# Feed-forward layers: a ranked queue behind every six matmuls, no GpSimd there, and attention heads in another order

## The chip, the cores and the metric

The kernel runs on one core of one Trainium2 chip. Its time is the device time of one execution in microseconds (us); a time shown without more is the median of three executions. Everything else comes from one profiled execution of the same program.

## The reference

The kernel computes a masked attention and then two feed-forward layers on its output. `q`, `k` and `v` are 2 x 8 heads x 768 x 64; the mask lets a query see only keys of the same sign bucket.

```python
    mask = q_bucket[:, :, :, None] == k_bucket[:, :, None, :]
    scores = scale * np.matmul(q, k.transpose(0, 1, 3, 2))
    scores = np.where(mask, scores, -1000000000.0)
...
    x = np.ascontiguousarray(attn_out.transpose(0, 2, 1, 3)).reshape(B * S, H * D)
...
    h = x @ w_in                                   # 1536 x 512 @ 512 x 2048
    g = h * (1.0 / (1.0 + np.exp(-1.702 * h)))     # layer 0; layer 1: h * tanh(softplus(h))
    return (g @ w_out).astype(np.float32)          # 1536 x 2048 @ 2048 x 512
```

## The kernel before

**Attention** is a software pipeline of 96 steps (16 heads x 6 query tiles of 128). A step holds, in a fixed order, transposes of the probabilities, the mask's clamp on VectorE, the exponential on ScalarE, the next step's scores and the product with `v`; a dictionary `todo` adds work at given steps. GpSimd prepares each head's operands. When a pair of heads is done, `x_out` (GpSimd) writes its 128 features into `xq`. `norm0` (GpSimd), `norm0b` (VectorE's reciprocal), `norm1` (a TensorE transpose), `norm2` and `norm3` (DMAs) bring a head's row sums to `x_out`. The batches are the token halves; the heads come in order 0 to 15, so that the last batch's pairs of features come as 0, 1, 2, 3.

**Feed-forward** (`moe`) holds f32 values as a high part rounded for the fast matmul format plus a low part, and takes three matmuls (high x high, high x low, low x high) for one product. The tokens are cut in three blocks of 512. Block r goes straight through; the other two, c = 0 and 1, share a Winograd-like scheme: seven products for a 2 x 2 block product in place of eight. Its left factors come from `xq` (`xfactors`: `b11`, `t1`, `t2`, `b21`, `t3`, `b22`, `t4`, each for e = 0, 1 and each split in high and low), its right ones from the weights (`ssums`, `ssplit`: four sums of quarters of the weight tiles, then their split).

The 2048 hidden features are taken in 16 tiles f, two to a pair p. The work on TensorE for a pair comes in units of six matmuls of 512 columns: R1 (four units: hidden tile of block r), R2 (four: its output tiles), Q1 (seven products, each a unit) and Q2 (eight output tiles of blocks 0 and 1), so 23 units or 138 matmuls for a pair and 16 pairs in two layers. After Q1 or R1 come activations on ScalarE, each computed twice (rounded `gh`, full), and `gl`, their difference. An output tile is added to `yr` or `xq` (L749), which frees its PSUM bank, one of three.

The weights arrive as 64-bit words, one tile of 512 KB for each (layer, f, in or out), by the DMA queue of SyncE into three buffers. `wsplit` turns a tile into f32 and splits it: ScalarE (L136, L138), VectorE's shift (L140) and its merge (L143; in layer 1 two instructions, L145 and L146), ScalarE's rounding (L158), and the low part (L160).

All of this is written out by hand, without a scheduler: every engine executes its instructions in the order of the program and waits in place for what the next one needs. Around each group of units `run` spreads a list of background steps evenly over the units, first the units' own hooks and then as many background steps as divide the list evenly. GpSimd does in feed-forward: the low parts of the weights (L160), `ssums` and the low part of `ssplit` (L191), one of seven recombinations of Q1 (`h1`, L815, which also needs a copy by ScalarE, L814), one of four `gl` of Q1 (L725), `xr_lo` (L752), and half of `xfactors`.

The order of a pair from the third on is Q1, R2, R1 of the next pair, Q2. Between the layers all of `xfactors` for both e is put in one block behind R1 of layer 1's first pair.

## Time and profile before

| | |
|---|---|
| median of three executions | 795.69 us (794.42 to 796.49) |
| the profiled execution's own time | 793.73 us |
| its span, first to last instruction | 791.8 us |
| mean granted clock of TensorE | 0.984 |
| busy: TensorE, VectorE, ScalarE, GpSimd | 94%, 67%, 54%, 52% |

Engines are named PE (TensorE), PEld (its weight loads), DVE (VectorE), ACT (ScalarE), POOL (GpSimd) and SP (the DMA queue of SyncE). L749 is line 749 of the kernel. A row of a timeline has start (us from the span's start), duration (us), engine, line, operation, output<-inputs, shape and, in brackets, how long the engine had been idle before it and what ended that. A row of groups has the count, busy us in all, mean ns of one, and after the bar the idle us before them with what ended it. A row of stretches has the stretch, its length, the busy us of PE, PEld, DVE, ACT and POOL (instructions in brackets), the granted clock (1.00 is 2.4 GHz, 0.50 is 1.2 GHz) and the DMA engines' share and rate. Some records of matmuls are missing, and a matmul's end is modelled, so that back-to-back matmuls overlap in the rows.

### The profile page before, as it was taken

How to read it: one execution, taken by the hardware profiler on the slowest of the kernel's cores; microseconds unless marked ns; L12 is line 12 of the kernel's file. 1: busy time of each engine (PE TensorE's matmuls, PEld its weight loads, DVE VectorE, ACT ScalarE, POOL GpSimd, SP SyncE). 2: the span in 40 equal slices, each digit the busy share in tenths (PEclk: the TensorE clock that was granted, in tenths of full speed). 3: DMA queues.
4: the chain of work that ended last, by engine and by line, in shares of the span. 5: the costliest groups of instructions: out<-in, count | busy, mean ns of one | idle time of the engine just before them, and what ended most of it. 6: DMA issues, size and time to landing. Idle time of an engine off the chain costs nothing.

```text
span 791.8 us, 10720 instructions
## 1 busy us (share of the span) xinstructions
PE 745.6 (94%) x3688; PEld 632.8 (80%) x3688; DVE 529.9 (67%) x920; ACT 429.7 (54%) x859; POOL 410.3 (52%) x375
## 2 busy tenths in 40 slices
PE   8999999999998899999999999739989999999998
PEld 7999999999976687778787787527867877778786
DVE  8888888988987625555465545685555657566464
ACT  7888888888885453443434433454433443343421
POOL 8867877788555533424434345474433442434520
PEclk9999999999999999999999999979999999999999
DMA  6666667666332111121121211201111112121004
GB/s 166 171 159 154 155 158 177 164 157 165 98 99 85 49 60 53 40 94 54 54 80 54 81 53 54 92 14 53 55 53 53 60 47 81 54 79 54 27 0 160
DMA packets 25911, 69.60 MB, mean 88 GB/s; under 512 B 4448, under 2 KB 6720, under 8 KB 25856
## 3 DMA queue, kind: packets, MB, share of 16 engines
q1 hardware_dynamic: 25856, 68.91, 30.1%
q8 instruction: 29, 0.48, 0.2%
q14 instruction: 26, 0.21, 0.1%
HBM read 49.19 MB, written 3.19 MB: 66 GB/s over the span
## 4 chain that ended last, share of the span: by engine, by line
PE 61%; DVE 12%; ACT 11%; POOL 8%; issue 8%; DMA 0%; SPq 0%; DVEq 0%; POOLq 0%; ACTq 0%
PE y L737 20%; PE s L448 8%; PE pt L509 8%; PE h L242 5%; PE W L783 4%; PE u L534 4%; PE u L533 4%; PE Y L783 3%; ACT gh L722 2%; PE X L783 2%; DVE gl L725 2%; PE prep L357 2%; POOL wl L160 2%; DVE raw L140 1%; DVE wb L143 1%
## 5 line engine op out<-in xcount | busy, mean ns | idle before, releaser
L160 POOL TENSOR_TENSOR wl<-wb,wh 128x512 fp32r<-128x512 f32 x60 | 79.1, 1319 | 100.2 <-ACT wh L158 100.2
L521 DVE TENSOR_TENSOR ptl<-pt,pth 128x384 fp32r<-128x384 f32 x192 | 98.2, 552 | 24.6 <-ACT pth L516 23.7
L516 ACT CAST pth<-pt 128x384 fp32r<-128x384 f32 x192 | 83.0, 484 | 29.4 <-PE pt L509 29.2
L737 PE MATMUL y<-wh,gh 128*128 128x512 f32 x192 | 77.5, 404 | 21.5 <-ACT yr L747 12.3
L749 DVE TENSOR_TENSOR xq<-xq,y 128x512 f32<-128x512 f32 x112 | 75.0, 684 | 30.4 <-PE y L737 29.1
L472 ACT ACTIVATE p<-p,mn 128x768 f32<-128x768 f32 x96 | 91.1, 949 | 2.3 <-DVE p L461 2.2
L461 DVE TENSOR_SCALAR_CACHE_REDUCE p<-s 128x768 f32<-128x768 f32 x96 | 90.5, 944 | 0.8 <-PE s L448 0.7
L158 ACT CAST wh<-wb 128x512 fp32r<-128x512 f32 x64 | 39.5, 617 | 91.4 <-DVE wb L143 47.0
L725 POOL TENSOR_TENSOR gl<-r,gh 128x512 fp32r<-128x512 f32 x16 | 20.7, 1295 | 128.8 <-ACT r L723 128.8
L737 PE MATMUL y<-gh,wh 128*128 128x512 f32 x192 | 77.1, 402 | 9.4 <-DVE xq L749 6.6
L509 PE MATMUL pt<-ident,p 128*128 128x128 f32 x576 | 80.9, 274 | 0.4 <-ACT p L472 0.3
L737 PE MATMUL y<-gh,wl 128*128 128x512 f32 x192 | 76.3, 397 | 1.8 <-DVE wl L160 1.8
L737 PE MATMUL y<-gl,wh 128*128 128x512 f32 x192 | 76.0, 396 | 0.0
L737 PE MATMUL y<-wh,gl 128*128 128x512 f32 x192 | 76.0, 396 | 0.0
L737 PE MATMUL y<-wl,gh 128*128 128x512 f32 x192 | 75.8, 395 | 0.0
L509 PEld LDWEIGHTS pt<-ident,p 128*128 128x128 f32 x576 | 68.3, 140 | 7.1 <-ACT p L472 1.5
L715 DVE TENSOR_TENSOR gl<-h,gh 128x512 fp32r<-128x512 f32 x32 | 22.0, 690 | 70.7 <-ACT h L714 70.7
L533 PE MATMUL u<-pth,vv 128*128 128x384 f32 x192 | 64.9, 338 | 0.0
L534 PE MATMUL u<-ptl,vv 128*128 128x384 f32 x192 | 64.9, 338 | 0.0
L737 PEld LDWEIGHTS y<-wh,gh 128*128 128x128 f32 x192 | 36.7, 191 | 34.8 <-ACT yr L747 12.7
L448 PE MATMUL s<-kh,qx 128*128 128x384 f32 x192 | 55.4, 369 | 0.4 <-DVE p L461 0.4
L815 POOL TENSOR_TENSOR r<-s,s 128x512 f32<-128x512 f32 x16 | 23.1, 1443 | 62.1 <-ACT s L814 62.1
(198 smaller groups left out, 1892.2 us busy)
## 6 DMA issues: line engine op xcount, KB each, us to landing
raw<-in_wt_dram SPq DMA_DIRECT2D x64, 512.0 KB
kn<-in_kt_dram SPq DMA_DIRECT2D x15, 384.0 KB
qn<-in_qt_dram SPq DMA_DIRECT2D x16, 192.0 KB
vn<-in_vt_dram SPq DMA_DIRECT2D x8, 384.0 KB
ul<-uh SPq DMA_DIRECT2D x16, 192.0 KB
rb<-scr SPq DMA_DIRECT2D x16, 192.0 KB
qx<-qk_m SPq DMA_DIRECT2D x15, 192.0 KB
qb<-qk_m SPq DMA_DIRECT2D x15, 192.0 KB
```

What stands on the lines that cost most here:

```text
L160: sub(lo, wf, rnd(hi))
L448: nc.tensor.matmul(s[:, f, :HS], a[:, c], bb[:, f * HS : (f + 1) * HS], start=st, stop=not st,)
L461: nc.vector.tensor_scalar(sb, s[:, :, :HS], NEG, None, ALU.min, ALU.min, accum_out=mn)
L472: nc.scalar.activation(p, p, AF.Exp, bias=mn, scale=-1.0, accum_out=z_t[n][:, t : t + 1],)
L509: nc.tensor.transpose(ptile[:, j * P : (j + 1) * P], p_t[3 * g + j][:, t * P : (t + 1) * P], ident,)
L516: nc.scalar.copy(hi, ptile[:, :HS])
L521: nc.vector.tensor_sub(lo, ptile[:, :HS], rnd(hi))
L533: nc.tensor.matmul(ut[:, :HS], vv[:, t, :], hi, start=(t == 0), stop=False)
L534: nc.tensor.matmul(ut[:, :HS], vv[:, t, :], lo, start=False, stop=(t == NT - 1))
L737: nc.tensor.matmul(y, w[:, js] if m == 0 else x[:, js], x if m == 0 else w, start=(n == 0), stop=(n == 5),)
L749: nc.vector.tensor_add(acc, acc, y)
L783: nc.tensor.matmul(bk[b], w[:, k], x[:, e], start=(first and n == 0), stop=(n == 5), skip_group_check=True,)
```

## The change

- The order on TensorE is one list, `walk`, of 63 groups and 364 units (R1 of layer 0's first pair lies in attention, as before). From the third pair on it is Q1, R1 of the next pair, R2, Q2.
- All else in feed-forward goes into a heap `due`, keyed by the unit at which it is due, a rank, and the order of entry. After each unit everything due by then is written out. What hangs on the unit itself has rank 1 (`fold`, which is L749 and its kin, and `c0` to `c6`), `gl` has rank 2 and comes one unit later than the activations, weights, sums and x factors have rank 3.
- `wlist`, the order in which weight tiles are loaded and converted, is sorted by the units at which they are wanted (`LEAD` units ahead, or when the buffer comes free). `wsplit` takes four units for a tile.
- No instruction of GpSimd is left in feed-forward (`POOLW` is empty): what it did goes to VectorE. `c1` adds straight from PSUM, so the copy L814 goes.
- `xfactors` of layer 1 is spread over units: e = 0 from the fourth unit of the first layer's last Q2, e = 1 ten units later.
- `UO` makes the last batch's pairs of features come as 0, 2, 1, 3. So e = 0 is complete one pair sooner, and eleven more of its steps are put on GpSimd in steps 85 to 93; the e = 1 steps that are possible before the last pair move from steps 85 to 93 to steps 93 to 95, `x_out` of the seventh pair from step 95 to 92, `ssums` and `ssplit` of the first pair four steps ahead, and the last head's `norm1`, `norm2` and `norm3` three steps ahead.

```diff
+    KCONV = 5
+    POOLW = ()
+    SU1 = 2
+    SLOT = {
+        ("t2h", 0): "qn", ("t2l", 0): "qn", ("b21h", 0): "kn", ("b21l", 0): "kn", ("t3h", 0): "vn",
+    }
+    LEAD = (15, 26)
...
+    nat = ctx.enter_context(tc.tile_pool(name="nat", bufs=2))
     tf = {}
-    for nm in ("b11", "t1"):
-        tf[nm] = [xpool.tile([P, 2, CH], F32R, name=f"{nm}{s}") for s in "hl"]
+    tpool = {}
+    UO = (0, 1, 2, 3, 4, 6, 5, 7)
...
+    def factor(nm, e):
+        if (nm, e) not in tf:
+            tf[nm, e] = []
+            for s in "hl":
+                tag = SLOT.get((nm + s, e))
+                if tag:
+                    t = nat.tile([P, S], F32R, tag=tag, name=nm + s, bufs=1 if tag == "vn" else 2)
+                    t = t[:, 0:CH]
+                else:
+                    early = nm in ("b11", "t1") or (e == 0 and nm + s in ("t3l", "b22h", "b22l"))
+                    pool = xpool if early else tpool["xt"]
+                    t = pool.tile([P, CH], F32R, name=f"{nm}{s}{e}")
+                tf[nm, e].append(t)
+        return tf[nm, e]
...
+    walk = []
     for m in range(2):
-        ps = [("i", 0), ("i", 1), ("o", 0), ("o", 1)]
+        if m == 1:
+            walk += [("R1", m, 0)]
+        walk += [("R1", m, 1), ("R2", m, 0), ("Q1", m, 0), ("R2", m, 1), ("Q2", m, 0)]
+        walk += [("Q1", m, 1), ("R1", m, 2), ("Q2", m, 1)]
         for p in range(2, NP):
-            ps += [("i", p), ("o", p)]
-        wlist += [(m, 2 * p + z, int(s == "o")) for s, p in ps for z in range(2)]
+            walk += [("Q1", m, p)]
+            walk += [("R1", m, p + 1)] if p + 1 < NP else []
+            walk += [("R2", m, p), ("Q2", m, p)]
...
+    N = {"R1": 4, "R2": 4, "Q1": 7, "Q2": 8}
...
+    order = [(0, f, j) for f, j in ((0, 0), (1, 0), (2, 0), (3, 0), (0, 1))]
+    rest = []
+    for m in range(2):
+        for f in range(KF):
+            for j in range(2):
+                if (m, f, j) not in order:
+                    u0 = mark["R2" if j else "R1", m, f // 2] - LEAD[j] + 3 * (f % 2)
+                    u0 -= 12 if (m, f // 2, j) == (1, 0, 0) else 0
+                    pm, pp = divmod(m * NP + f // 2 - 2, NP)
+                    free = mark["Q2" if j else "Q1", pm, pp] + 7 + j if pm >= 0 else 0
+                    if (m, f // 2, j) == (0, 1, 1):
+                        free = mark["Q1", 0, 0]
+                    if (m, f // 2, j) == (1, 1, 1):
+                        free = mark["R2", 1, 0]
+                    rest.append((max(free + f % 2, u0), (m, f, j)))
+    wlist = order + [t for _, t in sorted(rest)]
+    wtime = [0] * len(order) + [u for u, _ in sorted(rest)]
...
-        nc.gpsimd.tensor_add(sf[:, 0], a[2], a[3])
+        v = nc.gpsimd if (m, p) == (0, 0) else nc.vector
+        v.tensor_add(sf[:, 0], a[2], a[3])
         yield
...
-        nc.gpsimd.tensor_sub(sl, sf, rnd(sh))
+        v = nc.gpsimd if (m, p) == (0, 0) else nc.vector
+        v.tensor_sub(sl, sf, rnd(sh))
...
+            def head(n):
+                return divmod(2 * UO[n // 2] + n % 2, H)
             def load_q(n):
-                b, h = divmod(n, H)
+                b, h = head(n)
...
-                at(NT * (n + 1) + NZ, norm1, n)
-                at(NT * (n + 1) + NZ, norm2, n)
-                at(NT * (n + 1) + NZ + 2, norm3, n)
+                nz = NZ if n < NHD - 1 else NZL
+                at(NT * (n + 1) + nz, norm1, n)
+                at(NT * (n + 1) + nz, norm2, n)
+                at(NT * (n + 1) + nz + 2, norm3, n)
...
-            for e in range(2):
-                for n, op in enumerate(xfactors(e, pcopy, nc.gpsimd.tensor_sub, False)):
-                    at(2 * NT * (5 + e) + XO + 2 + 2 * n, op)
+            def x_ops(e, late, st, gap):
+                for n, op in enumerate(xfactors(e, pcopy, nc.gpsimd.tensor_sub, late)[:11]):
+                    at(st + int(n * gap), op)
+            x_ops(0, False, 2 * NT * 5 + XO + 2, 2)
+            x_ops(0, True, 2 * NT * 6 + XO + 2, 0.8)
+            x_ops(1, False, 2 * NT * 7 + XO - 2, 0.5)
             for n, g in enumerate((ssums, ssums, ssums, ssums, ssplit, ssplit)):
-                at(NSTEP - 8 + n, sgo, g, 0, 0)
+                at(NSTEP - 12 + n, sgo, g, 0, 0)
...
+            due = []
+            now = [0]
+            def at_unit(u, f, rank=3):
+                heappush(due, (u, rank, next(tick), f))
+            tick = count()
+            def after(d, f, rank=1):
+                at_unit(now[0] + d, f, rank)
+            def flush():
+                while due and due[0][0] <= now[0]:
+                    heappop(due)[-1]()
+            def gl_sub(gl, h, gh, sub=DV):
+                return lambda: sub(gl, h, rnd(gh))
...
-            def q_act(m, f, c, h, sub):
+                after(1, gl_sub(gl, h, gh), 2)
...
+                def fold():
+                    if p == 0:
+                        nc.scalar.copy(acc, y)
+                    else:
+                        nc.vector.tensor_add(acc, acc, y)
+                    if p == NP - 1 and m == 0 and c == "r":
+                        nc.scalar.copy(xr_hi[:, j], acc)
+                        after(2, lambda: DV(xr_lo[:, j], acc, rnd(xr_hi[:, j])), 2)
+                    if p == NP - 1 and m == 1:
+                        t0 = (0 if c == "r" else (c + 1) * CH) + j * P
+                        nc.sync.dma_start(out[t0 : t0 + P, :], acc)
+                after(1, fold)
...
+                        after(1, hook)
...
+                def c0():
+                    nc.scalar.copy(tmp("s1"), bk["W"])
+                def c1():
+                    add(tmp("r"), t["s1"], bk["Y"])
...
+                def c4():
+                    add(t["r"], t["r"], bk["X"])
+                    q_act(m, fb, 1, t["r"])
...
+            def conv(k, u0):
+                m, f, j = wlist[k]
+                for n, d in enumerate((0, 0, 1, 2, 3)):
+                    at_unit(u0 + d, lambda: wgo(k, 1, GP if wlist[k] in POOLW else DV))
+                    if n == 2:
+                        at_unit(u0 + d, lambda: wfetch(k + 4))
+            def sums(m, p, u0, u1):
+                for n in range(4):
+                    at_unit(u0 + n // 2, lambda: sgo(ssums, m, p))
+                for n in range(2):
+                    at_unit(u1 + n, lambda: sgo(ssplit, m, p))
...
+            for k in range(KCONV + 1, len(wlist)):
+                conv(k, wtime[k])
+            for m in range(2):
+                for p in range(m == 0, NP):
+                    u0 = max(0, mark["R1", m, p] - LEAD[0] + 5 - 12 * ((m, p) == (1, 0)))
+                    q1 = mark["Q1", m, p - 1] if p else mark["Q1", 0, NP - 1]
+                    if p == 1:
+                        u0 = mark["Q1", 1, 0] + 7 if m else SU1
+                    sums(m, p, u0, max(q1 + 7, u0 + 2))
+            def xf(e, steps, u0, hi, sub, rate):
+                ops = xfactors(e, hi, sub, False) + xfactors(e, hi, sub, True)
+                for n in range(steps, len(ops)):
+                    at_unit(u0 + (n - steps) // rate, ops[n])
+            xf(0, 16, 5, nc.scalar.copy, DV, 2)
+            at_unit(5, lambda: late.pop()())
+            xf(1, 5, 7, nc.scalar.copy, DV, 2)
+            u7 = mark["Q2", 0, NP - 1]
+            XT = (0, 1, 1, 2, 3, 3, 3, 4, 5, 5, 2, 3, 4, 5, 6, 7, 6, 7)
+            for e, u0 in ((0, u7 + 3), (1, u7 + 13)):
+                ops = xfactors(e, nc.scalar.copy, DV, False) + xfactors(e, nc.scalar.copy, DV, True)
+                for n, op in enumerate(ops):
+                    at_unit(u0 + XT[n], op)
...
+            at_unit(mark["R1", 1, 0], mish)
+            wgo(KCONV, 2, DV)
             r_act(0, 0)
+            wgo(KCONV, 1, DV)
             r_act(0, 1)
-            for op in xfactors(0, pcopy, GP, True):
-                op()
-            run(r_units(0, 1), r_hooks(0, 1), conv(0, 1, 1, DV))
-            run(out_units(0, 0, ("r",)), {}, conv2(0, 1, 1, GP)[:4] + [late.pop()])
-            es_u.close()
-            pools["gq"] = es.enter_context(tc.tile_pool(name="gq", bufs=1))
-            wo[1] = es.enter_context(tc.tile_pool(name="wo1", bufs=1))
-            for op in xfactors(1, nc.scalar.copy, DV, True):
-                op()
-            for m in range(2):
-                if m == 1:
-                    load_table(SET_MISH)
-                    wstate["mish"] = True
...
-                    run(out_units(m, 0, ("r",)), {}, conv2(m, 1, 1)[:4])
-                q_run(m, 0, conv2(m, 1, 1)[4:] + sums(m, 1, 0, 4))
-                run(out_units(m, 1, ("r",)), {}, sums(m, 1, 4, 6) + conv2(m, 2, 0)[:3])
...
+            at_unit(1, lambda: wgo(KCONV, 2, DV), 0)
+            for w in walk:
+                if w == ("Q1", 0, 0):
+                    es_u.close()
+                    pools["gq"] = es.enter_context(tc.tile_pool(name="gq", bufs=1))
+                    wo[1] = es.enter_context(tc.tile_pool(name="wo1", bufs=1))
+                for go in units(*w):
+                    go()
+                    now[0] += 1
+                    flush()
```

## Rows read from the trace of the kernel before

**Rows 1.** The page: the span in 40 slices, busy tenths, clock in tenths.

```profile
PE   8999999999998899999999999739989999999998
...
DVE  8888888988987625555465545685555657566464
...
PEclk9999999999999999999999999979999999999999
```

**Rows 2.** Stretches: the first pairs, one of each layer, and the layer change.

```profile
236.07:268.50 32.43, 27.06 (x109) 21.11 (x109) 23.66 (x32) 17.77 (x33) 17.52 (x17) 0.95 0.25 82
388.25:420.70 32.45, 31.92 (x138) 25.75 (x138) 17.57 (x30) 13.16 (x24) 12.89 (x12) 1.00 0.19 65
485.53:550.80 65.27, 47.54 (x187) 37.61 (x187) 43.22 (x51) 31.45 (x55) 40.70 (x33) 0.87 0.15 49
676.47:709.97 33.50, 32.18 (x139) 25.67 (x139) 20.93 (x34) 13.28 (x24) 13.39 (x12) 1.00 0.18 63
```

**Rows 3.** Waits of PE, 236 to 788: us in all, times, longest.

```profile
PE y L737 <- ACT yr L747: 12.3, 1, 12.3
PE y L737 <- DVE xq L749: 9.3, 3, 5.3
PE y L737 <- DVE yr L749: 9.0, 14, 1.2
PE X L783 <- DVE q L818: 3.3, 1, 3.3
PE y L737 <- DVE wl L160: 1.8, 1, 1.8
PE h L242 <- ACT zt L497: 1.6, 1, 1.6
```

**Rows 4.** Timeline of PE and DVE at the end of the span.

```profile
780.33 0.39 PE L737 MATMUL y<-wh,gl 128*128 128x512 f32 x1
...
787.81 0.39 PE L737 MATMUL y<-wh,gl 128*128 128x512 f32 x1
788.23 0.69 DVE L749 TENSOR_TENSOR xq<-xq,y 128x512 f32<-128x512 f32 x1 [0.67 <-PE y L737]
```

**Rows 5.** Timeline of ACT ahead of the 5.3 us wait.

```profile
495.98 1.04 ACT L189 CAST sh<-sf 128x1024 fp32r<-128x1024 f32 x1 [7.39 <-POOL sf L181]
```

**Rows 6.** Timeline of DVE, merges of weight words with GpSimd busy and idle.

```profile
497.62 2.38 DVE L143 SCALAR_TENSOR_TENSOR wb<-wb,raw 128x512 uint32<-128x512 uint32 x1 [5.54 <-ACT wb L136]
...
554.55 2.44 DVE L145 SCALAR_TENSOR_TENSOR raw<-wb,raw 128x512 uint32<-128x512 uint32 x1 [1.37 <-ACT wb L138]
...
596.88 0.69 DVE L145 SCALAR_TENSOR_TENSOR raw<-wb,raw 128x512 uint32<-128x512 uint32 x1 [1.51 <-ACT wb L138]
```

**Rows 7.** Groups of DVE over the whole span.

```profile
L715 DVE TENSOR_TENSOR gl<-h,gh 128x512 fp32r<-128x512 f32 x32 | 22.0, 690 | 70.7 <-ACT h L714 70.7
...
L725 DVE TENSOR_TENSOR gl<-X,gh 128x512 fp32r<-128x512 f32 x16 | 11.1, 692 | 18.5 <-ACT X L723 18.5
L725 DVE TENSOR_TENSOR gl<-W,gh 128x512 fp32r<-128x512 f32 x16 | 11.1, 692 | 27.7 <-ACT W L723 27.7
...
L818 DVE TENSOR_TENSOR q<-s,X 128x512 f32<-128x512 f32 x16 | 11.0, 687 | 27.7 <-PE X L783 27.4
...
L579 DVE TENSOR_TENSOR xq<-ul,rb 128x256 f32<-128x256 f32 x1 | 0.4, 418 | 0.0
```

**Rows 8.** Groups of POOL from 250 to 790.

```profile
L160 POOL TENSOR_TENSOR wl<-wb,wh 128x512 fp32r<-128x512 f32 x58 | 76.5, 1320 | 98.4 <-ACT wh L158 98.4
```

**Rows 9.** Timeline of POOL at the end of attention.

```profile
221.57 1.83 POOL L558 TENSOR_TENSOR ul<-ul,uh 128x768 f32<-128x768 f32 x1
...
225.55 0.20 POOL L484 TENSOR_SCALAR z<-z 128x6 f32<-128x6 f32 x1
```

**Rows 10.** Timeline of DVE there.

```profile
229.96 0.17 DVE L487 RECIPROCAL z<-z 128x6 f32<-128x6 f32 x1
```

**Rows 11.** Timeline of SP there.

```profile
213.99 0.47 SPq L504 DMA_DIRECT2D rb<-scr  x1
```

More of the change, by code (lines that the diff above doesn't have):

```diff
@@ L1 @@
 from contextlib import ExitStack
+from heapq import heappop, heappush
+from itertools import count
 import numpy as np
@@ L768, in q_part, with go, q_units @@
+                after(1, fold)
+            def r_units(m, p):
+                def go(f, k):
+                    r_in(m, f, k, k + 2)
+                    if k == 2:
+                        after(1, lambda: r_act(m, f))
+                return [lambda f=f, k=k: go(f, k) for f in (2 * p, 2 * p + 1) for k in (0, 2)]
+            def q_units(m, p):
                 fa, fb = 2 * p, 2 * p + 1
[L769 to L770 removed]
@@ L771, in q_part, with tmp, product @@
                 bk = {}
-                def product(b, lhs, off, nm, first, last):
+                t = {}
+                def tmp(nm):
+                    t[nm] = cs.tile([P, CH], F32, tag=nm, name=nm)
+                    return t[nm]
+                def product(b, lhs, off, nm, first, last, hook):
                     def go():
@@ L854, in two @@
-            def two(a, b):
-                r = []
-                for n in range(7):
-                    r += a[n : n + 1] + (b[n - 2 : n - 1] if n >= 2 else [])
-                return r
-            def conv2(m, p, j, sub=nc.gpsimd.tensor_sub):
-                return two(conv(m, 2 * p, j, sub), conv(m, 2 * p + 1, j, sub))
-            def sums(m, p, n0=0, n1=6):
-                gs = (ssums,) * 4 + (ssplit,) * 2
-                return [lambda g=g: sgo(g, m, p) for g in gs[n0:n1]]
-            def run(units, hooks, bg):
-                bg = list(bg)
-                for n, u in enumerate(units):
-                    u()
-                    for h in hooks.get(n, ()):
-                        h()
-                    left = len(units) - n
-                    for _ in range(-(-len(bg) // left)):
-                        bg.pop(0)()
@@ L877, in q_run, with A, Bw, Sm @@
-            def q_run(m, p, bg):
-                units, hooks = q_part(m, p)
-                run(units, hooks, bg)
-            DV = nc.vector.tensor_sub
-            GP = nc.gpsimd.tensor_sub
+                def A():
+                    return w_t[m, fa, 0]
+                def Bw():
+                    return w_t[m, fb, 0]
+                def Sm():
+                    return [s.rearrange("p a b -> p (a b)") for s in s_t[m, p]]
+                def add(o, a, b):
+                    nc.vector.tensor_add(o, a, b)
@@ new lines, in out_units, with units @@
+            def out_units(m, p, cs_, js):
+                return [lambda c=c, j=j: out_tile(m, p, c, j) for c, j in zip(cs_, js)]
+            def units(kind, m, p):
+                if kind == "R1":
+                    return r_units(m, p)
+                if kind == "Q1":
+                    return q_units(m, p)
+                if kind == "R2":
+                    return out_units(m, p, "r" * KD, range(KD))
+                if m == 0 and p == NP - 1:
+                    return out_units(m, p, (0, 1) * KD, (0, 0, 2, 2, 1, 1, 3, 3))
+                return out_units(m, p, (0,) * KD + (1,) * KD, list(range(KD)) * 2)
@@ new lines, in moe @@
+            at_unit(1, lambda: wgo(KCONV, 2, DV), 0)
+            for w in walk:
+                if w == ("Q1", 0, 0):
[6 more added lines that the diff above has]
+                    flush()
+            now[0] += 100
+            while due:
+                flush()
```

154 lines of the change are left out of this document (46 added, 108 removed).

## The prediction

> **What bounds the kernel now.** I read the page first, the span in forty slices [rows 1]. In the first twelve slices (attention) PE, DVE and ACT are all nearly full; from there on PE still stands at 9, while DVE falls to 4 to 6. So feed-forward, some 550 of 792 us, is bound by TensorE, and the question is how much of its time is not matmuls. The two low slices, 7 and 3, and the clock's only 7 lie in one place.
>
> The price of a matmul comes from an undisturbed stretch at the end: from 780.33 to 787.81 there are 34 matmuls in a row, so (787.81 - 780.33) / 33 = 0.2267 us from start to start [rows 4]. A unit of six costs 1.36 us, a pair of 138 costs 31.3. R1 of the first pair lies in attention, so 15 x 24 (R1) + 16 x 24 (R2) + 16 x 42 (Q1) + 16 x 48 (Q2) = 2184 matmuls are left: 495.1 us.
>
> The stretches [rows 2] show what is lost against that. The first pairs (108 matmuls, 24.5 us) take 32.43: 7.9 lost. A regular pair of layer 0 takes 32.45 (1.2 lost), of layer 1 33.50 (2.2 lost). The change of layers (186 matmuls, 42.2 us) takes 65.27: 23.1 lost. With no loss at all: PE could start R1 at 236.07 - 1.6 = 234.47 [rows 2, 3], would end at 234.47 + 495.1 = 729.6, and what follows the last matmul now (787.81 + 0.23 to the span's end at 791.8, 3.8 us) makes 733.4. That is the floor of the span, 58.4 below 791.8.
>
> The waits [rows 3] say whom PE waits for: 37.3 us that the profile marks, the rest being start-ups behind each wait and a granted clock under 1 in the first pairs (0.95) and at the layer change (0.87) [rows 2]. In each case it is an engine with time to spare whose queue holds the wanted instruction behind another. The 5.3 us wait for `xq` is the example: the addition stood behind a weight merge (497.62), which had been idle 5.5 us for ACT; ACT had been idle 7.4 us for a sum of GpSimd [rows 5, 6].
>
> **The change part by part.**
>
> *Work taken from GpSimd.* Per pair VectorE gets four low parts of weights, the low part of the sums, one `gl` and `c1`, and four sums. On GpSimd one two-input instruction of 128x512 takes 1.32 us [rows 8]; on VectorE it takes 0.69, one of 128x256 0.42 [rows 7]. 128x1024 on VectorE isn't in the trace: at least one, at most two of 128x512; I take two, 1.38. Sum: 4 x 0.69 + 1.38 + 2 x 0.69 + 4 x 0.42 = 7.2 us. A regular pair has 17.57 us of DVE in layer 0 and 20.93 in layer 1 [rows 2], so 24.8 and 28.1 under a PE pair of 31.3: hidden, with 6.5 and 3.2 to spare. ACT loses a copy; at 13.3 it stays far below. Cover gone, each us over 31.3 would cost a us in every pair.
>
> What GpSimd's leaving gives back: the merge L145 took 2.44 us at 554.55 and 0.69 at 596.88 [rows 6]. The Trainium skill, "SBUF — State Buffer", Who interferes with whom, says that a VectorE instruction with two SBUF inputs and a GpSimd one that reads SBUF exclude each other for whole instructions. By it the slow cases would all go; here that only widens the spare time, and I count nothing for it.
>
> *Order by rank.* The additions that free PSUM come first behind each unit, `gl` a unit later, so that it stands behind nothing that ACT still has to make; R1 now lies between Q1 and R2, 5.4 us in which VectorE can finish Q1's tail. The repeated waits for `yr` and `X` should go. I leave 0.2 us a pair: 3 in all (bounds 0, and 2.2 a pair in layer 1, the second rival).
>
> *First pairs.* The late x factors of e = 0 are made in attention; those of e = 1 follow `x_last` from the seventh unit on, two steps a unit. In the seven units of the first Q1 I count on VectorE five additions, three `gl`, five steps of x factors, two merges and two low parts (17 x 0.69) and a shift (0.42): 12.2 us for 9.5 of PE. An excess of 2.7 delays the factors, which PE wants one unit after they are due. I take 3 us (bounds 0.3 and the 7.9 of before).
>
> *Layer change.* Before, ACT's 14 rounded copies stood in one block ahead of the copy L747 that frees a bank: the 12.3 us. Spread, the 22 VectorE steps (15.2 us at 0.69) have 20 units (27.2 us) beside eight additions (5.5); the densest place has four of them and an addition behind one unit, 3.5 us against 1.4, and three PSUM banks give two units of delay. Once PE no longer stands still, the half clock there has no cause either. I take 2 us (bounds 0, and half of 23.1).
>
> *Attention's end.* The 96 steps keep their instructions on PE, DVE and ACT. On GpSimd `x_out` of the seventh pair comes earlier, but not before its DMA (issued at 213.99 [rows 11]) has landed; behind it stand seven steps of x factors, at most 7 x 1.32 = 9.2, then the addition to the last head's sums (225.55), for which VectorE's reciprocal (229.96) waits, and behind that the transposes' low parts and so PE. `x_out` takes 4.0 (221.57 to 225.55) [rows 9, 10]. Started at 217, 3 us behind the issue, an estimate, GpSimd is through at 230.2 and VectorE waits 0.2; started at 221.57 as before it waits 4.8. I take 0.5 (bounds 0 and 4.8). `norm1` three steps sooner removes PE's 1.6 us for `zt`, which the floor holds already. The DMAs are the same in number; on SP the last head's `norm3` still stands behind weight loads that wait for merges, so I count no gain from it.
>
> Sum of the span: 733.4 + 3 + 3 + 2 + 0.5 = 741.9. The profiled execution's own time is 1.9 above its span and the median another 2.0 above that (795.69 against 793.73): 745.8.
>
> **The rivals.**
>
> *VectorE becomes the bound of layer 1.* For it: 28.1 of 31.3 is 90%, and VectorE waits in place for others. Against it: GpSimd's slowing of it is gone. If the pairs of layer 1 stay at 33.5, 8 x (2.2 - 0.2) = 16: 762. The Trainium skill, "Perfetto Trace Analysis", Optimizing Scalar/DVE Operations, speaks for this one: where VectorE is saturated it would move work to ScalarE or even GpSimd, the reverse of this change; the same sentence doubts that it helps between those two, since they share a read port. No row here has VectorE at 90% in feed-forward.
>
> *The handovers keep half of their loss.* If a late x factor still stops PE at the layer change and its clock falls, as in [rows 2], half of 23.1 stays in place of 2: 755. For it: each factor is due one unit ahead of its use. Against it: in layer 1's first Q1 they come in over 20 units.
>
> *Slower.* VectorE's waits stay in its queue, now with no time to spare. Per pair it is idle before `gl` of R1 2 x 70.7 / 32 = 4.4 us, of X and of Y 18.5 / 16 = 1.2 each (Y has X's figure), of W 1.7, and before `q` 1.7 [rows 7]: 10.2. Were all of these to stand, pairs would take 24.8 + 10.2 = 35.0 and 38.3 us: 8 x 3.7 + 8 x 7.0 = 85.6 over the floor, 733.4 + 85.6 + 5.5 + 3.9 = 828. It decides from a mean pair of 31.3 + (795.7 - 742.8) / 16 = 34.6 us on, 742.8 being the floor with the other terms. Against it: these idle times are waits with nothing else queued, and the queue now puts other work there.
>
> *It doesn't do what it says*: PE waits as long elsewhere, 795. No row speaks for it but that several queues in order can always hold each other.
>
> **How the numbers follow.** I give my forecast 0.68, layer 1 bound by VectorE 0.17, the handovers 0.09, slower 0.04, no change 0.02. The time is that of the first, 746. Its own range goes from the floor's 737.3 with the least bounds (0.3), 738, to 733.4 + 3.9 + 7.9 + 6 + 3 + 1.5 = 756. To leave no more than 2 in 10 out it reaches to the second case: 738 to 764. Faster by over 0.3% (about what a measurement of this kernel can tell from no change) 0.94, within it 0.02, slower 0.04.
>
> **What the profile after would show.** Right: POOL empty from about slice 12 on; PE at 9 in every slice of feed-forward; regular pairs of 31.3 to 31.6 us in both layers; the granted clock at 1.00 across the layer change; DVE at 24 to 28 us a pair, its instructions at 0.69. Wrong: waits of PE for `q`, `r` or `xq` in every pair of layer 1 with DVE full in front of them (the first rival); a gap in the first Q1 or behind the last Q2 of layer 0, with the clock down (the second); PE idle at 228 to 236 for the reciprocal (attention's end).

## The result, and the profile after

The changed kernel takes 742.01 us (median of 4 runs, 741.94 to 742.11), the kernel before beside it 796.09 us: a ratio of 0.9315, 95% interval 0.9282 to 0.9348, so 54 us less. The prediction said 746, with a range of its own from 738 to 756.

The page of the changed kernel: the busy times, and four lines of the forty slices (each 18.5 us long here; feed-forward begins in the thirteenth).

```profile
PE 729.5 (99%) x3688; PEld 630.2 (85%) x3688; DVE 599.9 (81%) x1099; ACT 424.0 (57%) x844; POOL 186.1 (25%) x193
...
PE   8999999999999999999999999999999999999997
...
DVE  8888889988887958787687867988597797978754
...
POOL 7867877887893000000000000000000000000000
PEclk9999999999999999999999999999999999999999
```

Against [rows 1] the hole in PE's line and the 7 of its clock are gone, POOL is empty after attention, and DVE stands mostly at 6 to 9 where it stood mostly at 4 to 6.

Stretches of the changed kernel (columns as in [rows 2]): the first pairs, regular pairs of layer 0, the change of layers, regular pairs of layer 1.

```profile
234.79:267.03 32.24, 30.93 (x133) 24.43 (x132) 27.54 (x49) 22.27 (x40) 0.00 (x0) 1.00 0.35 106
...
377.19:408.47 31.28, 31.28 (x139) 25.90 (x138) 23.92 (x40) 12.90 (x23) 0.00 (x0) 1.00 0.21 68
469.00:533.00 64.00, 62.33 (x269) 49.73 (x268) 52.94 (x90) 36.08 (x63) 0.00 (x0) 1.00 0.16 50
600.16:631.45 31.29, 31.29 (x140) 25.90 (x139) 26.07 (x45) 12.83 (x22) 0.00 (x0) 1.00 0.20 68
```

A regular pair is 138 x 0.2267 = 31.28 us of matmuls: both layers now lose nothing, where [rows 2] had 32.45 and 33.50. Around the change of layers PE was busy for 47.54 of 65.27 us before; now it is for 62.33 of 64.00, at a granted clock of 1.00 (2.4 GHz) in place of 0.87. (The two stretches are about equally long and don't hold the same work.)

The waits of PE in feed-forward of the changed kernel: us in all, times, longest. Two more, of 0.2 us each, for `yr` and `xq`, follow below these.

```profile
PE W L877 <- DVE b21l L257: 1.3, 1, 1.3
PE h L302 <- DVE gl L796: 0.8, 1, 0.8
PE X L877 <- DVE q L900: 0.4, 1, 0.4
...
```

That is 2.9 us in five waits, where [rows 3] had 37.3. L826, L877, L302, L840, L796, L900 and L257 are the output tile's matmul, Q1's products, R1's products, the fold (L749 before: the addition of an output tile), `gl`, the recombinations and the x factors' low parts. The steps of `wsplit` stand in L193 and L195 (ScalarE), L197 (shift), L200, L202 and L203 (merges), L215 (ScalarE's rounding) and L217 (low part); L250 is the low part of the sums. Groups of DVE from 230 us on show where the queue itself waits:

```profile
L796 DVE TENSOR_TENSOR gl<-h,gh 128x512 fp32r<-128x512 f32 x32 | 21.8, 683 | 2.2 <-ACT h L803 2.2
L250 DVE TENSOR_TENSOR sl<-sf,sh 128x1024 fp32r<-128x1024 f32 x15 | 18.4, 1224 | 0.7 <-ACT sh L247 0.7
...
L202 DVE SCALAR_TENSOR_TENSOR raw<-wb,raw 128x512 uint32<-128x512 uint32 x26 | 17.8, 684 | 0.4 <-ACT wb L195 0.2
...
L796 DVE TENSOR_TENSOR gl<-X,gh 128x512 fp32r<-128x512 f32 x16 | 11.0, 688 | 4.5 <-ACT X L812 4.5
...
L796 DVE TENSOR_TENSOR gl<-W,gh 128x512 fp32r<-128x512 f32 x16 | 10.9, 682 | 0.0
```

Before `gl` of R1 VectorE stood idle for 70.7 us in all, before that of W for 27.7 and of X for 18.5 [rows 7]; now for 2.2, nothing and 4.5. A `gl` issued one unit after its activations mostly finds them done. The merges (L202) take 0.68 us, none 2.4 as in [rows 6].

### The profile page after: what moved, and what is told of

It reads as the page before. It is cut to its first block, busy times and chain, and to the rows that moved or that the text cites. A ratio compares the mean times of both kernels' runs of the same rounds, so it can differ in the third digit from the quotient of the medians.

```text
span 740.3 us, 10663 instructions
## 1 busy us (share of the span) xinstructions
PE 729.5 (99%) x3688; PEld 630.2 (85%) x3688; DVE 599.9 (81%) x1099; ACT 424.0 (57%) x844; POOL 186.1 (25%) x193
## 4 chain that ended last, share of the span: by engine, by line
PE 86%; DVE 9%; ACT 2%; issue 1%; DMA 1%; SPq 0%; ACTq 0%; DVEq 0%
PE y L826 31%; PE h L302 9%; PE s L510 9%; PE pt L571 8%; PE X L877 8%; PE W L877 5%; PE Y L877 5%; PE u L596 4%; PE u L595 4%; PE prep L419 2%; DVE gl L796 1%; ACT p L534 1%; DVE xq L840 1%; DVE wl L217 1%; ACT pth L578 1%
## 5 line engine op out<-in xcount | busy, mean ns | idle before, releaser
L215 ACT CAST wh<-wb 128x512 fp32r<-128x512 f32 x64 | 39.7, 620 | 99.4 <-DVE wb L200 54.8
L840 DVE TENSOR_TENSOR xq<-xq,y 128x512 f32<-128x512 f32 x112 | 75.8, 683 | 17.1 <-PE y L826 16.0
L826 PE MATMUL y<-gh,wh 128*128 128x512 f32 x192 | 75.1, 391 | 0.5 <-DVE yr L840 0.2
L826 PE MATMUL y<-wh,gh 128*128 128x512 f32 x192 | 74.8, 390 | 0.2 <-DVE xq L840 0.2
L826 PE MATMUL y<-gh,wl 128*128 128x512 f32 x192 | 74.7, 389 | 0.0
L826 PE MATMUL y<-wl,gh 128*128 128x512 f32 x192 | 74.7, 389 | 0.0
L826 PE MATMUL y<-gl,wh 128*128 128x512 f32 x192 | 74.7, 389 | 0.0
L826 PE MATMUL y<-wh,gl 128*128 128x512 f32 x192 | 74.7, 389 | 0.0
L510 PE MATMUL s<-kb,qb 128*128 128x384 f32 x192 | 50.1, 340 | 1.2 <-ACT kb L474 1.2
L302 PE MATMUL h<-xr_hi,wh 128*128 128x512 f32 x128 | 50.0, 390 | 0.8 <-DVE gl L796 0.8
L302 PE MATMUL h<-xr_hi,wl 128*128 128x512 f32 x128 | 49.9, 390 | 0.0
L302 PE MATMUL h<-xr_lo,wh 128*128 128x512 f32 x128 | 49.8, 389 | 0.0
L217 DVE TENSOR_TENSOR wl<-wb,wh 128x512 fp32r<-128x512 f32 x62 | 42.4, 686 | 6.8 <-ACT wh L215 6.0
```

The source lines that it names most:

```text
L302: nc.tensor.matmul(h, a[:, wk], x[:, kk], start=(n == 0), stop=(n == 3 * KD - 1))
L510: nc.tensor.matmul(s[:, f, :HS], a[:, c], bb[:, f * HS : (f + 1) * HS], start=st, stop=not st,)
L826: nc.tensor.matmul(y, w[:, js] if m == 0 else x[:, js], x if m == 0 else w, start=(n == 0), stop=(n == 5),)
L840: nc.vector.tensor_add(acc, acc, y)
```

## The experiments

The theory: the gain is one of order. TensorE stopped because what it wanted stood in an engine's queue behind an instruction that waited for another engine; the new order takes these waits out (`gl` a unit later, PSUM's additions first, x factors spread). The rival: the gain is GpSimd's leaving, and the order only tidies up. All kernels are the changed one with the edit shown, unless said otherwise, and are timed against the kernel before.

**gpsimd_back.** GpSimd gets its old work of feed-forward back inside the new queue (the x factors, the recombination `c1` and the first pair apart).

```diff
-    POOLW = ()
+    POOLW = [(m, f, j) for m in range(2) for f in range(16) for j in range(2)]
-        v = nc.gpsimd if (m, p) == (0, 0) else nc.vector
+        v = nc.gpsimd
...
-                    q_act(m, fb, 1, t["r"])
+                    q_act(m, fb, 1, t["r"], GP)
...
-                        after(2, lambda: DV(xr_lo[:, j], acc, rnd(xr_hi[:, j])), 2)
+                        after(2, lambda: GP(xr_lo[:, j], acc, rnd(xr_hi[:, j])), 2)
```

> The new queue, with GpSimd given back what it did per pair in feed-forward (low parts of the weights and of the sums, the sums, one gl, xr_lo), all at the same units as now. Theory 'order' (the waits went because what frees TensorE stands first in its engine's queue): these instructions are wanted units later, so GpSimd's 1.32 us in place of 0.69 is hidden; regular pairs stay at 31.3 to 31.6 us, the time at 742 to 750 us. Theory 'GpSimd' (the waits came from its slow instructions and from VectorE being held up by them, 2.4 us for a merge of 0.69): waits come back in most pairs, 1 us and more in each, 758 us or more.

747.25 us, ratio 0.9370: 5.2 us more than the changed kernel, so some 49 of the 54 us stay with GpSimd at work. Groups of DVE and of POOL in feed-forward of this kernel:

```profile
L197 DVE TENSOR_SCALAR raw<-raw 128x512 uint32<-128x512 uint32 x59 | 36.9, 626 | 0.0
L200 DVE SCALAR_TENSOR_TENSOR wb<-wb,raw 128x512 uint32<-128x512 uint32 x34 | 32.3, 949 | 6.1 <-ACT wb L193 5.8
```

```profile
L217 POOL TENSOR_TENSOR wl<-wb,wh 128x512 fp32r<-128x512 f32 x58 | 77.1, 1329 | 123.5 <-ACT wh L215 123.5
L250 POOL TENSOR_TENSOR sl<-sf,sh 128x1024 fp32r<-128x1024 f32 x15 | 36.5, 2434 | 26.0 <-ACT sh L247 23.7 <-issue 2.3
```

A merge (L200) has a mean of 949 ns in this kernel, and about 685 in the changed one; 1.33 and 2.43 us of GpSimd become 0.69 and 1.22 on VectorE. A regular pair of layer 1 loses 0.5 us, nearly all the rest lies at the change of layers.

**old_queue_no_gpsimd.** The kernel before, its order untouched, with GpSimd's work of feed-forward on VectorE, and the copies of the x factors on ScalarE (the one change the rival needs).

```diff
-        nc.gpsimd.tensor_sub(sl, sf, rnd(sh))
+        v = nc.gpsimd if (m, p) == (0, 0) else nc.vector
+        v.tensor_sub(sl, sf, rnd(sh))
...
-                    nc.scalar.copy(tmp("s5"), bk["Y"])
-                    nc.gpsimd.tensor_add(tmp("r"), t["s1"], t["s5"])
+                    nc.vector.tensor_add(tmp("r"), t["s1"], bk["Y"])
...
-            def conv(m, f, j, sub=nc.gpsimd.tensor_sub):
+            def conv(m, f, j, sub=nc.vector.tensor_sub):
```

> The kernel before, its order as it was, but all that GpSimd did in feed-forward given to VectorE (the recombination straight from PSUM, without ScalarE's copy; the x factors of e = 0 to ScalarE and VectorE). Theory 'order': VectorE's idle waits of some 10 us a pair stay in its queue and 7 us of work are added, so the time gets no better than before: 790 to 830 us. Theory 'GpSimd': most of the gain comes with this alone, 745 to 770 us.

845.79 us (839.74 to 853.88), ratio 1.0578: slower than the 797.93 of before beside it, by that ratio by 46 us, past even the theory's range; the rival's is missed by some 75. Waits of PE in this kernel:

```profile
PE y L739 <- DVE yr L751: 42.3, 15, 3.5
PE y L739 <- ACT yr L749: 11.1, 1, 11.1
```

L739, L751 and L749 are this kernel's output tile, its additions and its copies. The first line stood at 9.0 us before, 14 times and 1.2 at most [rows 3]: an addition that frees a PSUM bank now comes up to 3.5 us late, once in nearly every pair. The second is the change of layers of [rows 3], 12.3 us there.

**old_queue_no_gpsimd_gl_later.** The same, with each `gl` written out one unit behind its activations.

```diff
-                nc.vector.tensor_sub(gl, h, rnd(gh))
+                pend.append(lambda: nc.vector.tensor_sub(gl, h, rnd(gh)))
...
-                return lambda: sub(gl, h, rnd(gh))
+                pend.append(lambda: sub(gl, h, rnd(gh)))
+                return lambda: None
...
+                    old, pend[:] = list(pend), []
                     u()
                     for h in hooks.get(n, ()):
                         h()
+                    for g in old:
+                        g()
```

> The old queue without GpSimd (846 us) with one more change, each gl one unit behind its activations. If gl's place decides whether VectorE can carry GpSimd's work: its idle waits of some 10 us a pair go, regular pairs fall by 2 to 4 us, 780 to 805 us, while the layer change and the first pairs stay as they were. If the rest of the queue's order decides: 825 us or more.

778.76 us, ratio 0.9771. The longest wait of PE, and one stretch of 100 us in layer 0, of this kernel:

```profile
PE h L244 <- DVE gl L718: 17.8, 1, 17.8
```

```profile
380.00:480.00 100.00, 100.00 (x443) 82.69 (x441) 74.67 (x128) 42.73 (x74) 0.00 (x0) 1.00 0.21 69
```

L244 and L718 are R1's products and `gl` in this kernel. The place of `gl` alone takes some 65 us off and turns 46 us slower into 18 us faster. In layer 0 PE then has no gap in 100 us, and a pair of layer 1 takes 31.64 us (621.31 to 652.95), 0.4 over its matmuls. So the regular pairs' gain needs neither the ranks nor the pair's new order: with GpSimd gone, `gl`'s place gives nearly all of it. What stays is mostly one wait, 17.8 us behind the block of x factors at the change of layers, and the first pairs.

**gl_at_once.** The other way round: the changed kernel with `gl` right behind its activations.

```diff
-                after(1, gl_sub(gl, h, gh), 2)
+                gl_sub(gl, h, gh)()
```

> The kernel after, with each gl put right behind its two activations in place of one unit later. If gl's place is what took VectorE's idle waits away: VectorE waits about 1.2 us for ScalarE before each of six gl in a pair, 7 us, and stands at 31 us in layer 0 and 33 in layer 1 against TensorE's 31.3, so some 2 us a pair in layer 1 and waits in Q1: 755 to 775 us. If VectorE has enough to spare (5 us of 31.3 in layer 1): 742 to 748 us.

815.55 us, ratio 1.0228: 74 us slower than the changed kernel and 18 slower than before. My expectation was far too low. The timeline of DVE at the end of a Q1 of layer 0 shows why:

```profile
351.40 0.68 DVE L900 TENSOR_TENSOR r<-r,X 128x512 f32<-128x512 f32 x1
353.44 0.69 DVE L796 TENSOR_TENSOR gl<-r,gh 128x512 fp32r<-128x512 f32 x1 [1.36 <-ACT r L812]
354.05 0.69 DVE L900 TENSOR_TENSOR Y<-q,Y 128x512 f32<-128x512 f32 x1
355.89 0.69 DVE L796 TENSOR_TENSOR gl<-Y,gh 128x512 fp32r<-128x512 f32 x1 [1.15 <-ACT Y L812]
...
363.81 0.69 DVE L796 TENSOR_TENSOR gl<-h,gh 128x512 fp32r<-128x512 f32 x1 [1.67 <-ACT h L803]
...
365.35 0.68 DVE L840 TENSOR_TENSOR yr<-yr,y 128x512 f32<-128x512 f32 x1
```

and that of ACT between:

```profile
352.11 0.63 ACT L811 ACTIVATE gh<-r 128x512 fp32r<-128x512 f32 x1 [1.35 <-DVE r L900]
...
354.77 0.60 ACT L811 ACTIVATE gh<-Y 128x512 fp32r<-128x512 f32 x1 [1.36 <-DVE Y L900]
```

The two engines take turns: VectorE recombines, waits for ScalarE to activate twice, takes `gl`, recombines, while ScalarE waits for it. A turn takes 2.45 us (353.44 to 355.89), and a unit of TensorE 1.36. R1's `gl` and the first fold come behind that lag, and PE waits for the fold from 363.31 to 366.09. One pair of each layer in this kernel (in the second the granted clock fell to 0.95, so part of its length is the clock's):

```profile
359.07:393.49 34.42, 31.64 (x140) 25.75 (x138) 23.51 (x41) 12.80 (x23) 0.00 (x0) 1.00 0.18 62
649.43:686.23 36.80, 33.27 (x140) 26.74 (x138) 26.21 (x45) 12.83 (x23) 0.00 (x0) 0.95 0.18 57
```

DVE is busy 23.51 us of 34.42, 68%, and still sets the length of the pair.

**no_ranks.** All background work has one rank, so that order of entry decides and weight steps come ahead of the folds of a unit.

```diff
-                heappush(due, (u, rank, next(tick), f))
+                heappush(due, (u, 0, next(tick), f))
```

> The kernel after with one rank for all: of what is due behind a unit, the weight steps and sums come first and the additions that free PSUM last. If the rank matters: c2 and c4 are late by one to three VectorE instructions (0.6 to 2 us) against one unit of slack (1.36 us minus their own 0.69), so TensorE waits up to 1 us in those pairs whose weight steps fall into Q1, and elsewhere the three banks cover it: 745 to 755 us. If what counts is only that work is due by units: 742 to 744 us.

765.99 us, ratio 0.9599: 24 us more, past the upper end. The timeline of DVE in a pair of layer 1, in which PE waited for `yr` from 617.59 to 619.35:

```profile
607.72 0.69 DVE L796 TENSOR_TENSOR gl<-r,gh 128x512 fp32r<-128x512 f32 x1 [1.36 <-ACT r L812]
...
610.17 0.69 DVE L796 TENSOR_TENSOR gl<-Y,gh 128x512 fp32r<-128x512 f32 x1 [1.15 <-ACT Y L812]
...
616.68 0.69 DVE L202 SCALAR_TENSOR_TENSOR raw<-wb,raw 128x512 uint32<-128x512 uint32 x1
617.41 0.69 DVE L203 SCALAR_TENSOR_TENSOR wb<-wb,raw 128x512 uint32<-128x512 uint32 x1
618.01 0.68 DVE L796 TENSOR_TENSOR gl<-h,gh 128x512 fp32r<-128x512 f32 x1
618.62 1.28 DVE L840 TENSOR_TENSOR yr<-yr,y 128x512 f32<-128x512 f32 x2
```

Two merges and a `gl` go ahead of the fold for which PE stands still. And the turn of gl_at_once is back, again 2.45 us (607.72 to 610.17): a `gl` entered earlier now goes ahead of the recombination of its unit, and VectorE waits in it. This run doesn't lead back to the kernel before, whose `run` wrote a unit's own additions ahead of its background steps too. It shows that the heap needs the rank, not that the rank is a part of the gain.

**x_block.** Layer 1's x factors in one block, due at one unit, as before.

```diff
-            for e, u0 in ((0, u7 + 3), (1, u7 + 13)):
-                ops = xfactors(e, nc.scalar.copy, DV, False) + xfactors(e, nc.scalar.copy, DV, True)
-                for n, op in enumerate(ops):
-                    at_unit(u0 + XT[n], op)
+            for c in (False, True):
+                for e in range(2):
+                    for op in xfactors(e, nc.scalar.copy, DV, c):
+                        at_unit(mark["R1", 1, 1], op)
```

> The kernel after, with all 36 steps of layer 1's x factors due at one unit, behind R1 of layer 1's first pair, as they stood before. Theory 'order': ScalarE's 14 copies and VectorE's 22 steps (13 us back to back) stand ahead of the copies that free the banks, TensorE stands still for some 8 to 12 us and its granted clock falls: 752 to 760 us. Rival (the old 12 us were GpSimd's slowness and its blocking of VectorE): with VectorE alone the block costs 3 us or less, up to 745 us.

759.09 us, ratio 0.9533: 17 us more, as the theory had it, in one wait of PE:

```profile
PE h L302 <- DVE gl L796: 16.6, 1, 16.6
```

**old_order.** Q1, R2, R1, Q2 as before.

```diff
-            walk += [("Q1", m, p)]
-            walk += [("R1", m, p + 1)] if p + 1 < NP else []
-            walk += [("R2", m, p), ("Q2", m, p)]
+            walk += [("Q1", m, p), ("R2", m, p)]
+            walk += [("R1", m, p + 1)] if p + 1 < NP else []
+            walk += [("Q2", m, p)]
```

> The kernel after, with a pair's groups in the order of before, R2 right behind Q1. If R1 in between is what took the waits for yr away: VectorE still has Q1's last addition and three gl to do when R2's first tiles come, TensorE waits 0.4 to 1.2 us a pair as before, 748 to 757 us. If the ranks alone do it: 742 to 745 us.

747.82 us, ratio 0.9386: between the two ranges, 6 us more than the changed kernel. The waits for `yr` that I expected don't come back (one of 0.2 us), so R1's new place isn't what took them away. PE waits a little for `q` in each Q1 instead: a pair takes 31.71 us in layer 0 (300.00 to 331.71) and 32.03 in layer 1 (587.86 to 619.89), 0.4 and 0.7 over its matmuls.

**heads_in_order.** `UO` is 0 to 7 in order; the late factors of e = 0 move into feed-forward, on GpSimd.

```diff
-    UO = (0, 1, 2, 3, 4, 6, 5, 7)
+    UO = (0, 1, 2, 3, 4, 5, 6, 7)
...
-            x_ops(0, True, 2 * NT * 6 + XO + 2, 0.8)
-            x_ops(1, False, 2 * NT * 7 + XO - 2, 0.5)
+            x_ops(1, False, 2 * NT * 6 + XO + 2, 2)
...
-            xf(0, 16, 5, nc.scalar.copy, DV, 2)
+            xf(0, 5, 1, pcopy, GP, 13)
```

> The kernel after with the heads in their old order, the late x factors of e = 0 made by GpSimd in feed-forward's first units as before, those of e = 1 at the old steps. By the working of the prediction the loss in the first pairs grows from 2.3 us (in the trace after) towards the 7.9 of before: 744 to 748 us. If the reordering only fills GpSimd's idle time and the factors were hidden anyway: 742 us.

747.84 us (745.49 to 751.84), ratio 0.9393: 3.4 to 6 us for the heads' order with what goes with it, GpSimd's work in the first units too, by the profiled execution and by the median. PE waits 2.6 us for R1's `gl` in the first R2.

**more_16** and **more_8.** How full may VectorE be? Each of the 12 regular pairs gets 16 or 8 idle additions of 128x512 at the lowest rank, spread over its units.

```diff
+            spare = xt.tile([P, CH], F32, name="spare")
+            nc.vector.memset(spare, 0.0)
+            for m in range(2):
+                for p in range(2, NP):
+                    for n in range(16):
+                        at_unit(mark["Q1", m, p] + 1 + n * 19 // 16, lambda: nc.vector.tensor_add(spare, spare, spare), 4)
```

> The kernel after with 16 idle additions of 128x512 put on VectorE in each of 12 regular pairs, at the last rank. VectorE's busy time in the trace after is 23.9 us (layer 0) and 26.1 (layer 1) of 31.3. At 0.69 each they are 11.0 us: 34.9 and 37.1, so pairs of at least that, 6 x 3.6 + 6 x 5.8 = 56 us more, 798 us. Back to back instructions start 0.60 apart in the trace: 9.6 us, 33.5 and 35.7 at most, 40 us more; and if the busy time itself counts overlaps twice, less than that. If VectorE were not near its bound: no change.

> Eight idle additions a regular pair in place of 16. With 16, a pair took 34.2 us in layer 0 and 36.9 in layer 1, which is VectorE's 23.9 and 26.1 plus 0.64 to 0.68 for each. If VectorE is the bound from that sum on: 8 x 0.66 = 5.3 give 29.2 (hidden) and 31.4, so 0 to 1 us a pair in layer 1, 742 to 749 us. If waits cost before it is full (half of the effect of 16): 765 us.

792.92 us with 16 (ratio 0.9955) and 757.57 with 8 (0.9504, between the two ranges). Stretches, one pair of each layer: first with 16, then with 8.

```profile
348.86:383.02 34.16, 32.38 (x140) 25.59 (x138) 32.59 (x57) 12.83 (x22) 0.00 (x0) 1.00 0.19 62
628.87:665.77 36.90, 32.73 (x139) 25.51 (x138) 35.35 (x61) 12.79 (x22) 0.00 (x0) 1.00 0.18 57
```

```profile
378.91:410.39 31.48, 31.48 (x139) 25.82 (x138) 27.74 (x49) 12.83 (x22) 0.00 (x0) 1.00 0.19 67
608.15:641.45 33.30, 31.85 (x140) 25.75 (x139) 30.52 (x53) 12.82 (x22) 0.00 (x0) 1.00 0.19 64
```

With 27.74 us of DVE a pair loses 0.2 us, with 30.52 it loses 2.0: with the additions placed so, the cover ends between these, before DVE's busy time reaches 31.3. With 8, one marked wait of 1.4 us stands in each of four pairs of layer 1, in the second stretch from 613.75 to 615.16. The profile puts it down to ScalarE's L195; the timeline of DVE in the kernel with 8 offers a nearer cause:

```profile
613.12 0.69 DVE L203 SCALAR_TENSOR_TENSOR wb<-wb,raw 128x512 uint32<-128x512 uint32 x1
613.73 0.69 DVE L1000 TENSOR_TENSOR spare<-spare 128x512 f32<-128x512 f32 x1
614.34 1.28 DVE L840 TENSOR_TENSOR yr<-yr,y 128x512 f32<-128x512 f32 x2
```

Two folds are done in a row, the first of them late behind a merge and an idle addition that an earlier unit had written out: a rank orders only what is due together, and what is in the queue can't be passed.

**spread_more.** An attempt at a better version: the two weight tiles wanted by the second pair of each layer three units later, layer 1's x factors one VectorE step a unit.

```diff
-                        free = mark["Q1", 0, 0]
+                        free = mark["Q1", 0, 0] + 3
-                        free = mark["R2", 1, 0]
+                        free = mark["R2", 1, 0] + 3
...
-            XT = (0, 1, 1, 2, 3, 3, 3, 4, 5, 5, 2, 3, 4, 5, 6, 7, 6, 7)
-            for e, u0 in ((0, u7 + 3), (1, u7 + 13)):
+            X0 = (0, 1, 2, 2, 3, 4, 5, 5, 6, 7, 6, 8, 7, 9, 8, 10, 9, 11)
+            X1 = (0, 1, 2, 2, 3, 4, 5, 5, 6, 7, 6, 7, 7, 8, 8, 9, 8, 10)
+            for e, u0, XT in ((0, u7 + 3, X0), (1, u7 + 12, X1)):
```

> The kernel after with the places of its remaining 6.3 us of waits thinned out: two pairs of weight conversions three units later, layer 1's x factors at about one VectorE step a unit (e = 1 from a unit sooner). If what remains is VectorE's local excess there: 2 to 5 us less, 737 to 740 us. If the waits only move: 741 to 743 us.

744.60 us, ratio 0.9350: slower than the changed kernel by 2.6. The waits of PE in this kernel that are new or longer:

```profile
PE y L826 <- DVE wl L217: 1.7, 2, 0.8
PE X L877 <- DVE q L900: 1.2, 1, 1.2
```

The wait for `b21l` is gone, and the low parts of the weights that were put back are late instead; the spread factors of layer 1 collide with the recombinations of its first Q1.

**x_rank.** The other remedy for the first pairs: their x factors at rank 2, ahead of the weight steps.

```diff
-                    at_unit(u0 + (n - steps) // rate, ops[n])
+                    at_unit(u0 + (n - steps) // rate, ops[n], 2)
```

> The changed kernel, with the x factors of layer 0's first pairs at rank 2 in place of 3, so that those due at a unit come ahead of the weight steps due there. If the 2.3 us lost in the first pairs is a matter of place in VectorE's queue (there a shift and two merges of weights, 0.42 + 2 x 0.69 us, stand ahead of b21's low part), TensorE's wait of 1.3 us for it shrinks to nothing or nearly, and the low parts of the weights, which come some 1 to 2 us later, are still in time: 739.5 to 741.5 us. If the first pairs hold too much VectorE work in any order, the wait moves on to the next factor or to a weight's low part, as it did in the run that put the same weights three units later: 741.5 to 744.

742.33 us (742.17 to 743.66), ratio 0.9324: no better. PE's wait for `b21l` falls from 1.30 us to 1.10, and one of 0.47 for `q` appears behind it. The timeline of DVE in this kernel:

```profile
247.96 0.69 DVE L257 TENSOR_TENSOR t2l<-xq,t2h 128x512 fp32r<-128x512 f32 x1 [0.74 <-ACT t2h L256]
...
248.90 0.69 DVE L271 TENSOR_TENSOR xq<-xq 128x512 f32<-128x512 f32 x1
249.51 0.68 DVE L200 SCALAR_TENSOR_TENSOR wb<-wb,raw 128x512 uint32<-128x512 uint32 x1
...
251.04 0.69 DVE L257 TENSOR_TENSOR b21l<-xq,b21h 128x512 fp32r<-128x512 f32 x1
```

The low part still comes only 0.36 us sooner than the changed kernel's (251.40), with a merge of an earlier unit still ahead of it. In the changed kernel DVE is busy for 11.42 of the first Q1's 11.82 us (245.69 to 257.51), whose matmuls take 9.52: it holds more VectorE work than one Q1 covers, and two ways of ordering it moved the loss without removing it.

## Why the prediction was right

The mechanism was the one predicted. Theory against rival: GpSimd's work back in the new queue costs 5 us of the 54; GpSimd's work gone from the old queue costs 46 more than before. The order carries the gain. By single undoing `gl`'s place is worth 74 us, the ranks 24, layer 1's spread factors 17, the pair's order 6, the heads' order 3 to 6, GpSimd 5. These don't add up to the gain. `gl`'s place is the part that both queues show, by 74 and by 65 us; the block of x factors costs one wait in each (16.6 and 17.8 us). The prediction named `gl`'s place, the ranks and R1's new place side by side; the runs put the weight on the first.

Step by step:

- *The floor, 733.4.* PE began R1 at 234.79 (234.47 predicted), the price of a matmul stayed 0.2267, and 234.79 + 495.1 + 6.3 of losses (below) leaves 4.1 us to the span's end (3.8). Right.
- *Work taken from GpSimd, 24.8 and 28.1 us of DVE a pair.* 23.92 and 26.07: hidden, as said. The 128x1024 subtraction took 1.22 us where I took 1.38, which makes 7.04 a pair; 17.57 + 7.04 - 23.92 = 0.7 and 20.93 + 7.04 - 26.07 = 1.9 remain. In layer 0 that is an error of the sum: the busy time of a stretch counts the overlap of two instructions once, and I added whole durations to it. Durations added up one by one grow by just these 7.0 us, from 18.83 in the stretch of [rows 2] to 25.86. In layer 1 they grow from 22.38 to 28.59, 0.8 less than that, which is the shift: 612 ns in the pair before, 422 after. The rest is overlap again. The merges of 2.4 us [rows 6] have no counterpart after, and a mean of 949 ns comes back with GpSimd: the trace agrees with the Trainium skill, "SBUF — State Buffer", Who interferes with whom. I counted nothing for it; gpsimd_back bounds it, with nearly all else of GpSimd's leaving, at 5 us.
- *Order by rank, 3 us left over 16 pairs.* Nothing is left: the regular pairs lose 0.0. Mis-sized by 3, and the reason given was in part wrong: the waits for `yr` stay away without R1 between Q1 and R2 (old_order).
- *First pairs, 3 us.* Their first Q1 runs from 245.69 to 257.51, 11.82 us for 42 matmuls of 9.52: 2.3. Right in place (the wait for a late x factor, `b21l`) and nearly in size.
- *Layer change, 2 us.* Summed in the same way over its groups of units, 4.0: its waits are 0.84, 0.36, two of 0.2 and two of 0.1, the rest start-ups around them. Mis-sized by 2. The clock stayed at 1.00, as said.
- *Attention's end, 0.5 us.* Right. The rows of POOL and of DVE there, in the changed kernel:

```profile
216.83 1.84 POOL L620 TENSOR_TENSOR ul<-ul,uh 128x768 f32<-128x768 f32 x1
...
228.22 0.26 POOL L546 TENSOR_SCALAR z<-z 128x6 f32<-128x6 f32 x1
```

```profile
230.00 0.18 DVE L549 RECIPROCAL z<-z 128x6 f32<-128x6 f32 x1
```

`x_out` began 0.2 us before the estimate of 217, GpSimd was through at 228.5, and the reciprocal stands at 230.00, without an idle time before it: the loss at R1's start against 234.47 is 0.3.

- *From span to time, 1.9 + 2.0.* The span of 740.3 was predicted at 741.9. The own time is 1.8 above it; the median is 0.1 below that. The 2.0 that the median of before lay above its profiled run didn't carry over, and it is the largest part of the 4 us by which 746 is too high. That the span came within 1.6 is in part luck: 3 too much for the pairs and 2 too little for the change of layers went against each other.

The rivals. *VectorE bounds layer 1*: refuted for this kernel, with nothing lost in its pairs, but not far off. Eight more additions a pair, 30.52 us of DVE, already cost 2.0 us a pair of layer 1, so time up to 31.3 isn't all to spare, as I took it to be. The Trainium skill's page "Perfetto Trace Analysis", Optimizing Scalar/DVE Operations, says that it may make sense to hand work of a saturated VectorE to others. At the fill of this kernel gpsimd_back, which does so with GpSimd, is 5 us slower; no run here does it at the fill of more_16.

*Slower*: the mechanism that I gave 0.04 is real. With `gl` at once the two pairs shown take 34.42 and 36.80 us (35.0 and 38.3 in that rival), their mean is past the 34.6 from which it was to decide, and the kernel takes 815.55 (828). So the outcome hung above all on `gl` a unit later, and the argument that "the queue now puts other work there" holds only with it, and only as long as the recombinations go ahead of it (no_ranks). My expectations of gl_at_once, no_ranks and old_queue_no_gpsimd were all too low; none of them reckoned with a turn between two engines that is longer than a unit and so adds up over the units of Q1. The rows show that turn in gl_at_once and no_ranks; for old_queue_no_gpsimd the 65 us of `gl`'s place speak for it.

*The handovers keep half*: x_block brings that case about, 17 us in one wait.

Left open: how the 5 us of gpsimd_back divide between slower merges and GpSimd's own longer instructions; what the new order of the weight tiles is worth, which no run undoes by itself; and what `gl` a unit later would give in the kernel before with GpSimd still at work, the smallest change of all, which no run tries.

## What to carry to other kernels

An engine at 68% can bound a loop: look, in the groups, for the idle time that stands before an instruction in an in-order queue and who ends it, and compare the turn between the two engines with the time that the bounding engine takes for a unit. Issue what depends on another engine one unit later than what produces it, and first what frees the bounding engine's buffers. Before taking work off a slow engine, mend the order: nearly the same move was 46 us slower in the old queue and 5 us faster in the new one.

## What the runs showed of the hardware

VectorE's records overlap: in a row the 128x512 instructions start 0.60 us apart (618.01 after 617.41 in no_ranks) while each lasts 0.69, so sums of durations overstate what a full queue takes. The busy time of a stretch counts such an overlap once: the 45 instructions in 26.07 us of the changed kernel's pair of layer 1 add up to 28.59. By that measure a pair lost 0.2 us at 27.74 of 31.3 and 2.0 at 30.52, with the additions of more_8. A 128x1024 subtraction took 1.22 us, less than two of 128x512. Beside a working GpSimd, in gpsimd_back, the 63 merges that no instruction of GpSimd overlaps took 0.69 us each, the 22 others 1.64 on average and 2.70 at most. And not only two-input instructions were slower: the shift L197, with one tile as input, had a mean of 626 ns there, 423 without and 756 with such an overlap, against 421 in the changed kernel:

```profile
L197 DVE TENSOR_SCALAR raw<-raw 128x512 uint32<-128x512 uint32 x61 | 25.7, 421 | 0.0
```
